# An attention-output stage put in a fixed order by hand, and snaps moved up in the down stage

## The chip, the cores and the metric

The kernel runs on one core of a Trainium2 chip. The metric is the device time of one execution in microseconds (us), lower is better. The timed figure is about 2 us more than the span of the profile of the same execution (757.7 against 755.9 for the kernel before), so spans are compared with spans and times with times. In the profile PE is TensorE (matrix multiplication), PEld its loading of weights, DVE is VectorE, ACT is ScalarE, POOL is GpSimd and SP is SyncE, which issues the data transfers (DMA).

## The reference, cut to what matters

```python
x = A_x                                   # 1 x 2048 x 1024, bf16
h = x + A(layernorm(x), wqkv, wo)         # attention block
out = h + B(layernorm(h), W_gate, W_up, W_down)

def A(x, wqkv, wo):                       # 32 heads of 32
    q, k, v = split(x @ wqkv)
    phi = lambda t: where(t > 0, t + 1, exp(t)) + 1e-6
    kv  = einsum("bhsd,bhse->bhde", phi(k), v);   z = sum(phi(k), s)
    num = phi(q) @ kv;   den = phi(q) @ z + 1e-6
    return concat_heads(num / den) @ wo

def B(x, Wg, Wu, Wd):                     # F = 3584
    g = x @ Wg;  h = relu(g) * (x @ Wu);  return h @ Wd
```

Attention is linear: for each token only a numerator and a denominator against one small matrix are needed, then a division, then the output projection.

## The kernel before

The large products (Q, K, V, gate, up, down) are done by the Strassen-Winograd scheme: seven products of half-size blocks in place of eight, with sums and differences of blocks on VectorE and copies of partial sums, here called snaps, that must be taken out of PSUM before TensorE may accumulate further into the same bank.

The attention-output stage works on 16 tiles of 128 tokens, in two halves of 8. For each tile it does the following steps.

- `nd`: 8 short matmuls of 132 columns, which yield numerators and denominators. They fill three PSUM banks, in pieces of 3, 3 and 2 matmuls.
- Ln and Exp on ScalarE give the reciprocal of the denominators, a multiplication on VectorE gives `o_sb` and so frees the bank.
- A DMA transposes `o_sb` into `oT`.
- `attn`: 16 matmuls of 512 columns, the output projection in two halves of 8. Each half needs one PSUM bank. VectorE adds the residual `x_res`.
- Layer norm on ScalarE, a DMA transpose of `hn`, and on VectorE the sums `hs` for Strassen.

The pool of PSUM banks is what ties these together: `nd` and `attn` share the same three banks (tag `"ab"`, `bufs=3`). The `nd` of one tile takes all three.

```python
    def strassen(pool, work, mm, fin, sbufs=3):          # a generator: 6 pieces
        ...
        for v in range(2):
            A[v] = pool.tile([P, NW], FP32, tag="A", bufs=2, name="Aq")
            mm(A[v], 1, v, True)
            snap(v, "m1")
        yield
        m2(0)
        for v in range(2):
            mm(A[v], 6, v, False)
            snap(v, "u2")
        m2(1)
        yield
        ...                                              # four more pieces

    def phi_end(dst, e):                                 # after phi_begin: dst = q + 1 + eps
        nc.scalar.activation(out=e, in_=dst, func=ACT.Exp, bias=negb[:, 0:1], scale=1.0)
        nc.vector.tensor_scalar(out=e, in0=e, scalar1=1.0, scalar2=PHI_EPS, op0=ALU.min, op1=ALU.add)
        nc.vector.tensor_tensor(out=dst, in0=dst, in1=e, op=ALU.max)

    # q_unit: one Exp, min and max for each 512 columns
        def fin(i, j, v, ps, m):
            dst = pqT[:, j * KH + c + v, i * HS + s * SW:i * HS + (s + 1) * SW]
            phi_begin(dst, ps, m)
            e = qw[-1].tile([P, NW], BF16, tag="e", name="e")
            phi_end(dst, e[:])

    # attn_stages(t)
        def nd():
            ...
            for c0, n in pieces:                         # 3, 3 and 2 of the 8
                ps = ndpool.tile([P, NW], FP32, tag="ab", name="nd")
                for c in range(c0, c0 + n):
                    nc.tensor.matmul(ps[:, (c - c0) * NDW:(c - c0 + 1) * NDW],
                                     lhsT=pqT[:, c, t * P:(t + 1) * P], rhs=kvz[:, c, :], start=True, stop=True)
                ...
                nc.scalar.activation(out=den[:, 0:n], in_=ndv[:, :, P:NDW], func=ACT.Ln, bias=deps[:], scale=1.0)
                nc.scalar.activation(out=rd[:, 0:n], in_=den[:, 0:n], func=ACT.Exp, scale=-1.0)
                nc.vector.tensor_tensor(out=ov[:, c0:c0 + n], in0=..., in1=rd..., op=ALU.mult)
        ...
        def wo_h():
            for j in range(2):
                ps = abpool.tile([P, NW], FP32, tag="ab", name="attn")
                for c in range(KC):
                    nc.tensor.matmul(ps[:], lhsT=st["oT"][:, c, :], rhs=wo_sb[:, c, j * NW:(j + 1) * NW],
                                     start=(c == 0), stop=(c == KC - 1))
                nc.vector.scalar_tensor_tensor(out=h_sb[:, j * NW:(j + 1) * NW], in0=ps[:], ...)   # residual
            ...                                          # layer norm

    for step in range(QSTEPS):                           # first half; Q of the second half between
        attn_step(step)
        ...
        for p in rest[step * len(rest) // QSTEPS:(step + 1) * len(rest) // QSTEPS]:
            next(p)
    ...                                                  # second half: pieces of four gate/up quads between

    # only here, ahead of the gate/up and down stages:
    ctx.enter_context(tc.manual_schedule(engines={ET.PE, ET.DVE, ET.Activation}))
```

The last line matters. Up to it the framework's scheduler decides the order of instructions on each engine; after it, the order of the program text is the order on TensorE, VectorE and ScalarE.

The down stage, which is in program order in both kernels, holds this (`pop()` issues one queued VectorE sum of operands for a later product, `s1`, `s2` and `s3` are the snaps, `prv` is the product before):

```python
            cur["m1"]()
            if prv:
                prv["11"]()
                pop()
            cur["s1"]()
            cur["m2"]()
            ...
            late_w()
            pop()
            cur["m6"]()
            if prv:
                prv["01"]()
            pop()
            ...
            cur["m5f" if tail else "m5"]()
            cur["s2"]()
```

Of the kernel before, what the change touches and what calls it, by code (L numbers as in the profile page):

```python
# [7 lines left out]
ACT = mybir.ActivationFunctionType  # L8
# [23 lines left out]
def block_kernel(ctx: ExitStack, tc: tile.TileContext, x, wqkv, wo, wg, wu, wd, out, H: int):  # L32
    nc = tc.nc
# [110 lines left out]
    def strassen(pool, work, mm, fin, sbufs=3):  # L144


        A, E, snaps = {}, {}, {}

        def snap(v, nm):
            if v == 0:  # L150
                snaps[nm] = work.tile([P, 2, NW], FP32, tag="snap", bufs=sbufs, name=nm)
            snaps[nm, v] = snaps[nm][:, v, :]
            nc.scalar.copy(out=snaps[nm, v], in_=A[v][:])  # L153

        def m2(v):
            d = pool.tile([P, NW], FP32, tag="D", bufs=1, name="Dq")
            mm(d, 2, v, True)
            fin(0, 0, v, d, snaps["m1", v])
# [4 lines that stand above are left out]
            snap(v, "m1")  # L163
        yield
        m2(0)
        for v in range(2):
            mm(A[v], 6, v, False)
            snap(v, "u2")
        m2(1)
        yield  # L170
        for v in range(2):
            E[v] = pool.tile([P, NW], FP32, tag="E", bufs=2, name="Eq")
            mm(E[v], 5, v, True)
        yield
        for v in range(2):
            mm(A[v], 7, v, False)
            snap(v, "u3")
            fin(1, 1, v, E[v], snaps["u3", v])
        yield
        for v in range(2):  # L180
            mm(A[v], 4, v, False)
            fin(1, 0, v, A[v], None)
        yield
        for v in range(2):
            mm(E[v], 3, v, False)
            fin(0, 1, v, E[v], snaps["u2", v])
        yield
# [242 lines left out]
    def q_unit(s, c):  # L430

        left = left_ops(xT[s], xS[s])
        ready = {}

        def mm(ps, m, v, start):
            for kc in range(KH):
                nc.tensor.matmul(ps[:], lhsT=rq[m - 1][:, kc, (c + v) * P:(c + v + 1) * P],
                                 rhs=left[m - 1][:, kc, :], start=(start and kc == 0),
                                 stop=(kc == KH - 1), skip_group_check=True)

        def fin(i, j, v, ps, m):
            dst = pqT[:, j * KH + c + v, i * HS + s * SW:i * HS + (s + 1) * SW]
            phi_begin(dst, ps, m)
            e = qw[-1].tile([P, NW], BF16, tag="e", name="e")
            phi_end(dst, e[:])

        return strassen(pspool, qw[-1], mm, fin)
# [47 lines left out]
    def attn_stages(t):  # L495
# [5 lines left out]
        def nd():  # L501
# [3 lines left out]
            ov = o_sb[:].rearrange("p (k h e) -> p k h e", k=KC, h=HPC)  # L505
            for c0, n in pieces:
                ps = ndpool.tile([P, NW], FP32, tag="ab", name="nd")
                for c in range(c0, c0 + n):
# [3 lines left out]
                den = bsmall.tile([P, GPB, HPC], FP32, tag="den", name="den")  # L512
                nc.scalar.activation(out=den[:, 0:n], in_=ndv[:, :, P:NDW], func=ACT.Ln, bias=deps[:], scale=1.0)
                rd = bsmall.tile([P, GPB, HPC], FP32, tag="rd", name="rd")
                nc.scalar.activation(out=rd[:, 0:n], in_=den[:, 0:n], func=ACT.Exp, scale=-1.0)  # L515
                nc.vector.tensor_tensor(  # L516
                    out=ov[:, c0:c0 + n], in0=ndv[:, :, 0:P].rearrange("p k (h e) -> p k h e", h=HPC),
                    in1=rd[:, 0:n, :].unsqueeze(3).to_broadcast([P, n, HPC, Dh]), op=ALU.mult)

        def oT():  # L520
            oT = bwork.tile([P, D], BF16, tag="oT", bufs=XB, name="oT")
            st["oT"] = oT[:].rearrange("p (c t) -> p c t", c=KC)
            nc.sync.dma_start_transpose(out=st["oT"], in_=st["o"][:])

        def x_in():
            x_sb = bwork.tile([P, D], BF16, tag="x_res", bufs=XB, name="x_res")
            nc.sync.dma_start(out=x_sb[:], in_=xf[t * P:(t + 1) * P, :])
            st["x"] = x_sb

        def wo_h():  # L530
            h_sb = st["x"]
            tot = bsmall.tile([P, 2], FP32, tag="tot", name="tot")
            for j in range(2):
                ps = abpool.tile([P, NW], FP32, tag="ab", name="attn")
                for c in range(KC):
                    nc.tensor.matmul(ps[:], lhsT=st["oT"][:, c, :], rhs=wo_sb[:, c, j * NW:(j + 1) * NW],  # L536
                                     start=(c == 0), stop=(c == KC - 1))
                nc.vector.scalar_tensor_tensor(out=h_sb[:, j * NW:(j + 1) * NW], in0=ps[:], scalar=1.0,  # L538
                                               in1=h_sb[:, j * NW:(j + 1) * NW], op0=ALU.mult, op1=ALU.add,
                                               accum_out=tot[:, j:j + 1])  # L540
            nc.sync.dma_start(out=h_dram[i][s][:, r // P, :], in_=h_sb[:])
            st["hn"] = bwork.tile([P, D], BF16, tag="hn", bufs=HB, name="hn")

            sm = bsmall.tile([P, 6], FP32, tag="sm", name="sm")
            nmean, var, lnv, rstd, nmr = (sm[:, i:i + 1] for i in range(5))
            nc.vector.tensor_scalar(out=nmean, in0=tot[:, 0:1], scalar1=tot[:, 1:2], scalar2=-1.0 / D,
                                    op0=ALU.add, op1=ALU.mult)
            nc.scalar.activation(out=st["hn"][:], in_=h_sb[:], func=ACT.Square, bias=nmean, scale=1.0, accum_out=var)
# [3 lines left out]
            nc.scalar.activation(out=st["hn"][:], in_=h_sb[:], func=ACT.Identity, bias=nmr, scale=rstd)  # L552

        def hn_T():
            nc.sync.dma_start_transpose(out=hnT[s][i][:, :, r:r + P], in_=st["hn"][:])

        return nd, oT, x_in, wo_h, hn_T

    LAG = (0, 1, 1, 2, 4)
    STS = ST // NS  # L560
    QSTEPS = STS + 0
    stages = [attn_stages(t) for t in order]
    begin_at = [n if n < STS else n - STS + QSTEPS for n in range(ST)]

    def attn_step(step):
        for k in range(len(LAG)):
            n = step - LAG[k]
            if n in begin_at:
                n = begin_at.index(n)
                stages[n][k]()  # L570
                if k == len(LAG) - 1 and n % STS >= NT:
                    left_sums(hnT[n // STS], hns[n // STS], slice(n % NT * P, (n % NT + 1) * P), nc.vector)

    rest = [p for s in range(1, NS) for c in range(0, KH, 2) for p in [q_unit(s, c)] * 6]
    for step in range(QSTEPS):
        attn_step(step)
        if step:
            for _ in range(-(-len(early_loads) // (QSTEPS - step))):
                early_loads.pop(0)(held[step][0:1, 0:1])
        for p in rest[step * len(rest) // QSTEPS:(step + 1) * len(rest) // QSTEPS]:  # L580
            next(p)
# [12 lines left out]
    def weight_sums(w_sb, fi, nm):  # L594
# [15 lines left out]
        return steps, lambda: (b[0][0], b[1][0], b[1][1], t[0][:, 3], t[0][:, 0], t[0][:, 1], t[0][:, 2])  # L610

    def run_sums(wt, fi):

        out = []
        for steps, ops in all_sums(wt, fi):
            for f in steps:
                f()
            out.append(ops())
        return out
# [66 lines left out]
    def early_quad(s, fc, w):  # L686
# [4 lines left out]
        def mm(ps, m, v, start):  # L691
            for kc in range(KH):
                nc.tensor.matmul(ps[:], lhsT=w[v][m - 1][:, kc, :], rhs=left[m - 1][:, kc, :],
# [16 lines left out]
        return strassen(pspool, mwork, mm, fin, 4)  # L710
# [5 lines left out]
    flow = []  # L716
    for f in range(NE):
        st = {}

        def begin(f=f, st=st):  # L720
            st["q"] = early_quad(0, f, run_sums(early[f // GP], f % GP))
            next(st["q"])

        flow += [begin] + [lambda st=st: next(st["q"])] * 5
    ready = STS + LAG[-1]
    for step in range(QSTEPS, ready):
        if step == QSTEPS:
            flow.pop(0)()
        attn_step(step)
    steps = QSTEPS + STS + LAG[-1] - ready  # L730
    for n in range(steps):
        attn_step(ready + n)
        for p in flow[n * len(flow) // steps:(n + 1) * len(flow) // steps]:
            p()
# [9 lines left out]
    ET = mybir.EngineType  # L744
    ctx.enter_context(tc.manual_schedule(engines={ET.PE, ET.DVE, ET.Activation}))

# [9 lines left out]
    def quad(s, fc, w, k):  # L756
# [10 lines left out]
        def m(n, nm, t=None):  # L767
# [3 lines left out]
            for v in range(2):  # L771
                for kc in range(KH):
                    nc.tensor.matmul(ps[:, v, :], lhsT=w[v][n - 1][:, kc, :], rhs=left[n - 1][:, kc, :],  # L773
# [89 lines left out]
    now = sums_of_run(0)  # L863
    for steps, _ in now:
        for f in steps:
            f()
    prv, k = None, 0
    for r, (wt, f, fi, toks) in enumerate(runs):
        w = [ops() for _, ops in now]
# [316 lines left out]
    for n in range(1, len(OUTER)):  # L1186
# [26 lines left out]
        if op["k"] in INNER:  # L1213
# [16 lines left out]
            pop()  # L1230
# [3 lines left out]
            pop()  # L1234
# [24 lines left out]
        else:  # L1259
            pss = []  # L1260
            for p in range(4):
                ps = acc(("A", "A", "XY"[(n + 1) % 2], "XY"[n % 2])[p])
                plain_mm(ps, n, p, 0)
                plain_mm(ps, n, p, 1)
                if p == 0 and prv:
# [7 lines left out]
                    load_h(op["k"], 1)  # L1273
                s, t0 = divmod(2 * p, NT)
# [4 lines left out]
                pop(2)  # L1279
# [50 lines left out]
```

## Time and profile before

| What | Kernel before |
|---|---|
| Time, median of 3 runs (range) | 755.6 us (755.51 to 757.81) |
| Span of the profile | 755.9 us, mean granted clock 0.993 |
| Attention-output stage, first `nd` to first gate/up quad after it | 147.2 to 298.0 us: 150.8 us |
| of which matmuls at their full pace | 592 x 0.2158 + 128 x 0.0592 = 135.3 us |
| of which lost | 15.4 us |

The pace comes from start to start of neighbouring matmuls in stretches without waits: 0.2158 us for 512 columns, 0.0592 us for 132 columns, 3.06 us for 28 of 256 columns. The end that the profile draws for a matmul is later than the start of the next, so a wait counted from start to start is 0.1 to 0.2 us longer than the idle time in brackets in the profile, and a group's length in the timeline is a little more than its cost.

The view of windows of the kernel before, by stage (attention output; gate/up quads; down). Columns are the window, its length, busy time and instruction count of each engine, then the granted TensorE clock, the DMA share and GB/s:

```profile
core 0: us, PE busy (x) PEld busy (x) DVE busy (x) ACT busy (x) POOL busy (x), PEclk, DMA share, GB/s
147.20:297.98 150.78, 139.48 (x707) 65.54 (x720) 113.37 (x293) 103.38 (x268) 1.50 (x8) 0.99 0.66 162
297.98:590.00 292.02, 290.75 (x1329) 132.35 (x1353) 221.53 (x406) 124.76 (x167) 0.00 (x0) 1.00 0.55 173
590.00:755.90 165.90, 157.10 (x1194) 118.55 (x1194) 127.45 (x108) 4.83 (x6) 0.00 (x0) 0.98 0.69 244
```

The middle stage has a clock of 1.00 and no gaps (290.75 of 292.02 us). The losses lie in the other two. The view of waits of TensorE in the kernel before says for what (total us, times, longest):

```profile
PE accA L1105 <- DVE snap L1111: 4.8, 2, 2.6
PE attn L536 <- DVE o_sb L516: 3.3, 7, 0.9
```

Two things in the timeline matter. First, how the attention stage hides the latency of the division (start, length, engine, line, operation, and in brackets the idle time before and its releaser):

```profile
155.74 0.63 PE L509 MATMUL nd<-kvz,pq_mem 128*128 128x132 bf16 x8
156.21 1.24 PE L437 MATMUL Aq<-xT,wq_sb 128*128 128x512 f16 x5
157.31 3.61 PE L536 MATMUL attn<-wo_mem,oT 128*128 128x512 bf16 x15
```

After the eight matmuls of `nd` the scheduler put five matmuls of Q (`Aq`), which need nothing of `nd`. When they are done a bank is free, and the projection starts with no wait. Secondly, the down stage has two gaps like this one:

```profile
626.73 4.88 PE L1105 MATMUL accA<-w,xd 128*128 128x256 f16 x28 [2.11 <-DVE snap L1111]
631.45 3.22 PE L1105 MATMUL accA<-wd,x 128*128 128x256 f16 x28
```

TensorE waits 2.11 us for the snap, and the 28 matmuls after the wait take 631.45 - 626.73 = 4.72 us from start to start in place of 3.06. They have the same form as the 28 after them; the clock is not the same (the view of windows gives 0.50 from 626.90 to 630.32 us, and 1.00 on both sides). The Trainium skill, "TensorE: Matmul & The Clock Gate", Part 1, says that a TensorE that was idle for a window of about 3.4 us runs at half rate, until it has been busy for about 3.4 us. The trace agrees with the half rate and with the time to warm up. The page (section "Wait — 56ns, not 53.3ns?") gives the cold pace as the number of columns over 1.2 GHz, which is 0.213 us for 256 columns by estimate, 0.104 us more than the measured 3.06 / 28 = 0.109. The excess of 4.72 - 3.06 = 1.66 us is then 16 slow matmuls, an estimate from that page's figure, and these take 16 x 0.213 = 3.4 us, as long as the trace's stretch at 0.50. The second such wait, near 732 us, was 2.64 us, with the same 4.72 us after it.

### The profile page before, as it was taken

The numbers are of one execution on the slowest core, as the hardware profiler recorded it, in microseconds if no ns is written. First come the engines' busy times: TensorE is split into PE (matmuls) and PEld (weight loads), VectorE is DVE, ScalarE is ACT, GpSimd is POOL, SyncE is SP. The second block draws the span as 40 slices with busy tenths as digits, with TensorE's granted clock in tenths as the row PEclk, the third lists the DMA queues.
The fourth block names the chain that finished last, engine by engine and source line by source line (L and its number), as shares of the span: only waits on it lengthen the run. The fifth ranks groups of instructions, "written<-read, shape, count | busy, mean of one in ns | idle before, by whom it ended". The sixth has DMA issues, their size and how long they took to land. (4 is left out here: it accounts for less than half of the span.)

```text
span 755.9 us, 10599 instructions
## 1 busy us (share of the span) xinstructions
PE 727.9 (96%) x3967; PEld 384.2 (51%) x4020; DVE 568.2 (75%) x1023; ACT 324.7 (43%) x596; POOL 5.9 (1%) x44
## 2 busy tenths in 40 slices
PE   8999999999889989999999999999999998999987
PEld 3444555444344434444444444444444477888556
DVE  6997654876886766778778787887776398995695
ACT  4785653878767644444344444434344110000000
POOL 0000000000000000000000000000000000000000
PEclk9999999999999999999999999999999999999999
DMA  9756003089857526165638368585482596987722
GB/s 321 167 125 153 0 1 112 1 188 218 186 144 178 135 74 202 35 185 140 200 110 237 112 194 252 194 253 179 144 302 96 189 385 244 360 295 281 238 98 56
DMA packets 146579, 132.03 MB, mean 175 GB/s; under 512 B 50912, under 2 KB 128096, under 8 KB 146528
## 3 DMA queue, kind: packets, MB, share of 16 engines
q1 hardware_dynamic: 135392, 123.23, 53.7%
q10 hardware_dynamic: 11136, 8.13, 3.4%
q8 instruction: 31, 0.51, 0.3%
q14 instruction: 20, 0.16, 0.1%
HBM read 79.95 MB, written 39.85 MB: 158 GB/s over the span
## 5 line engine op out<-in xcount | busy, mean ns | idle before, releaser
L783 ACT ACTIVATE gu<-gu 128x512 bf16<-128x512 bf16 x72 | 45.4, 630 | 131.7 <-DVE gu L782 127.3
L778 ACT COPY snap<-accA 128x1024 f32<-128x1024 f32 x72 | 72.4, 1008 | 37.1 <-PE accA L773 37.1
L536 PE MATMUL attn<-wo_mem,oT 128*128 128x512 bf16 x247 | 58.7, 385 | 4.1 <-DVE o_sb L516 3.3
L773 PEld LDWEIGHTS <-tg 128*128 128x128 f16 x384 | 37.6, 98 | 45.3
L773 PEld LDWEIGHTS <-tu 128*128 128x128 f16 x384 | 37.6, 98 | 45.3
L782 DVE TENSOR_TENSOR gu<-accY,snap 128x1024 bf16<-128x1024 f32 x36 | 43.9, 1219 | 9.8 <-ACT snap L778 9.8
L153 ACT COPY u<-Aq 128x512 f32<-128x512 f32 x56 | 32.3, 582 | 44.0 <-PE Aq L297 20.4
L782 DVE TENSOR_TENSOR gu<-accX,snap 128x1024 bf16<-128x1024 f32 x36 | 43.8, 1218 | 7.3 <-PE accX L773 4.7
L773 PE MATMUL accA<-hn,tg 128*128 128x512 f16 (+1 forms) x192 | 49.3, 379 | 0.0
L773 PE MATMUL accA<-hn,tu 128*128 128x512 f16 (+1 forms) x192 | 49.3, 379 | 0.0
L1105 PEld LDWEIGHTS <-x 128*128 128x128 f16 (+1 forms) x448 | 43.8, 98 | 5.5
L773 PEld LDWEIGHTS <-wg 128*128 128x128 bf16 x288 | 28.2, 98 | 34.9 <-issue 1.1
L773 PEld LDWEIGHTS <-wu 128*128 128x128 bf16 x288 | 28.2, 98 | 34.0
L536 PEld LDWEIGHTS <-oT 128*128 128x128 bf16 x256 | 25.3, 99 | 36.0 <-issue 8.5
L1105 PEld LDWEIGHTS <-xs 128*128 128x128 f16 x280 | 28.2, 101 | 6.7 <-issue 2.8
L297 PEld LDWEIGHTS <-xT 128*128 128x128 bf16 (+1 forms) x192 | 18.6, 98 | 24.5 <-issue 3.2
L786 DVE TENSOR_TENSOR hq<-gu 128x512 bf16<-128x512 bf16 x48 | 20.3, 422 | 14.3 <-ACT gu L783 14.2
L516 DVE TENSOR_TENSOR o_sb<-nd,rd 128x384 bf16<-128x384 f32 (+1 forms) x48 | 22.8, 506 | 8.6 <-ACT rd L515 7.5
L1111 DVE TENSOR_TENSOR snap<-accA,u 128x1024 f32<-128x1024 f32 x16 | 19.5, 1218 | 11.1 <-PE accA L1105 11.1
L538 DVE SCALAR_TENSOR_TENSOR x_res<-attn,x_res 128x512 bf16<-128x512 f32 x32 | 22.0, 688 | 7.6 <-PE attn L536 7.5
L934 PEld LDWEIGHTS <-x 128*128 128x128 bf16 (+1 forms) x168 | 16.4, 98 | 19.8
L773 PE MATMUL accA<-hn,wg 128*128 128x512 bf16 x73 | 23.3, 379 | 2.0 <-DVE gu L702 0.8
(232 smaller groups left out, 1417.0 us busy)
## 6 DMA issues: line engine op xcount, KB each, us to landing
x<-x_dram SPq DMA_DIRECT2D x17, 896.0 KB, 8.4
x_dram<-hq SPq DMA_DIRECT2D x28, 512.0 KB, 3.0
wg<-in_B_W_gate_dram SPq DMA_DIRECT2D x14, 512.0 KB, 5.2
wu<-in_B_W_up_dram SPq DMA_DIRECT2D x14, 512.0 KB, 7.5
wraw<-in_B_W_down_dram SPq DMA_DIRECT2D x14, 512.0 KB, 4.9
x_dram<-hq SPq DMA_DIRECT2D x28, 256.0 KB, 2.4
t_dram<-wt SPq DMA_DIRECT2D x28, 256.0 KB, 2.3
xd<-x_dram SPq DMA_DIRECT2D x6, 896.0 KB, 6.5
```

The costliest lines, as they stand in the source:

```text
L153: nc.scalar.copy(out=snaps[nm, v], in_=A[v][:])
L297: nc.tensor.matmul(ps[:], lhsT=left[m - 1][:, kc, r + v * P:r + (v + 1) * P], rhs=right[m - 1][:, kc, :], start=(start and kc == 0), stop= ...
L516: nc.vector.tensor_tensor(out=ov[:, c0:c0 + n], in0=ndv[:, :, 0:P].rearrange("p k (h e) -> p k h e", h=HPC), in1=rd[:, 0:n, :].unsqueeze(3 ...
L536: nc.tensor.matmul(ps[:], lhsT=st["oT"][:, c, :], rhs=wo_sb[:, c, j * NW:(j + 1) * NW], start=(c == 0), stop=(c == KC - 1))
L538: nc.vector.scalar_tensor_tensor(out=h_sb[:, j * NW:(j + 1) * NW], in0=ps[:], scalar=1.0, in1=h_sb[:, j * NW:(j + 1) * NW], op0=ALU.mult, ...
L773: nc.tensor.matmul(ps[:, v, :], lhsT=w[v][n - 1][:, kc, :], rhs=left[n - 1][:, kc, :], start=(t is not None and kc == 0), stop=(kc == KH - ...
L778: nc.scalar.copy(out=st[nm][:], in_=halves(st["A"]))
L782: add(out=g[:], in0=halves(st[nm]), in1=st[base][:], op=ALU.add)
L783: nc.scalar.activation(out=g[:, 0, :], in_=g[:, 0, :], func=ACT.Relu)
L786: add(out=out[q], in0=st[q][:, 0, :], in1=st[q][:, 1, :], op=ALU.mult)
L1105: nc.tensor.matmul(pv[:, tt, :], lhsT=left(m)[:, f, tt * P:(tt + 1) * P], rhs=right(m)[:, f, :], start=(t is not None and f == 0 and tt % ...
L1111: add(out=st[nm][:], in0=view("A"), in1=base[s][:, :, cols(j)], op=ALU.add)
```

## The change

Four things change, and all aim at TensorE's gaps.

1. The order of TensorE, VectorE and ScalarE is fixed by hand from the attention-output stage on, by a function `attn_steps`. Projection halves, pieces of Q and pieces of four gate/up quads alternate, and the Strassen pieces are finer (8 in place of 6).
2. The Exp of the reciprocal is one instruction for all three Ln of a tile, in place of three.
3. The phi of Q works on pairs of 512 columns: one Exp, min and max on 1024 columns.
4. In the down stage queued operand sums go behind the snap, and not ahead of it.

```diff
     def q_unit(s, c, fine=False):
...
-            dst = pqT[:, j * KH + c + v, i * HS + s * SW:i * HS + (s + 1) * SW]
-            phi_begin(dst, ps, m)
-            e = qw[-1].tile([P, NW], BF16, tag="e", name="e")
-            phi_end(dst, e[:])
+            pair = pqT[:, j * KH + c:j * KH + c + 2, i * HS + s * SW:i * HS + (s + 1) * SW]
+            phi_begin(pair[:, v], ps, m)
+            if v == 1:
+                e = qw[-1].tile([P, 2, NW], BF16, tag="e", name="e")
+                phi_end(pair, e[:])
... (nd)
-                nc.scalar.activation(out=den[:, 0:n], in_=ndv[:, :, P:NDW], func=ACT.Ln, ...)
-                nc.scalar.activation(out=rd[:, 0:n], in_=den[:, 0:n], func=ACT.Exp, scale=-1.0)
+                nc.scalar.activation(out=den[:, c0:c0 + n], in_=ndv[:, :, P:NDW], func=ACT.Ln, ...)
+                views.append(ndv)
+            nc.scalar.activation(out=rd[:], in_=den[:], func=ACT.Exp, scale=-1.0)
+            for (c0, n), ndv in zip(pieces, views):
                 nc.vector.tensor_tensor(out=ov[:, c0:c0 + n], ...
... (steps: "nd", "wo" by halves, "a" and "b" the layer norm, "h" the sums hs)
+    ctx.enter_context(tc.manual_schedule(engines={ET.PE, ET.DVE, ET.Activation}))
+
+    def attn_steps(n0, fills, between):
+        ...
+        for n in range(n0 + 1, n0 + STS):
+            do(n, "nd")
+            do(n - 2, "a")
+            do(n - 2, "b")
+            between(n - n0)
+            do(n - 1, "wo", 0)
+            fill()
+            do(n - 3, "h")
+            do(n - 1, "wo", 1)
+            extra = len(fills) - 4 - (n0 + STS - 1 - n)
+            fill(-(-extra // (n0 + STS - n)) if extra > 0 else 0)
...
+    stages[0]["nd"]()
+    for _ in range(4):
+        q_fill.pop(0)()
+    attn_steps(0, q_fill, early_load)
... (second half)
+    for _ in range(2):
+        flow.pop(0)()
+    stages[STS]["nd"]()
+    stages[STS - 1]["h"]()
+    for _ in range(2):
+        flow.pop(0)()
+    attn_steps(STS, flow, lambda n: None)
... (down stage)
             late_w()
-            pop()
+            if prv:
+                pop()
             cur["m6"]()
             if prv:
                 prv["01"]()
-            pop()
+                pop()
...
                 plain_mm(ps, n, p, 0)
-                plain_mm(ps, n, p, 1)
                 if p == 0 and prv:
                     prv["11"]()
 ...
+                    pop()
+                plain_mm(ps, n, p, 1)
...
-                pop(2)
+                pop(2 if p < 3 else 0)
```

## The prediction

> **What bounds it now.** TensorE: busy 727.9 of 755.9 us (the page). So only its gaps matter, and they lie in two places (timeline of TensorE). (1) Attention output, 147.2 to 298.0 us: at the measured pitches (0.216 us per 512-column matmul, 0.059 per 132-column one) its 592 + 128 matmuls are 135 us; the stage takes 150.7, so 15 us are lost. (2) The down stage: two waits for a VectorE "snap" (624.5 and 732.1 us). Each group after them (28 matmuls) takes 4.7 us instead of 3.06: the half-rate cold clock of the Trainium skill, "TensorE: Matmul & The Clock Gate", Part 1 (granted clock 0.91 and 0.93 in those windows). Together about 2.3 + 1.7 + 2.8 + 1.7 = 8.4 us.
>
> **Down stage.** Moving operand sums behind the snap lets the snap start when its matmuls end. I count both waits as gone: -8.4 us, VectorE keeping about 1 us of margin.
>
> **Attention stage.** The order is now strict on TensorE, VectorE and ScalarE. In it every nd (8 short matmuls, 0.47 us) is followed at once by half of an output projection, which needs a PSUM bank that the same nd has just filled (three banks, nd takes all three). In the trace nd to freed bank takes 1.6 to 1.9 us (Ln 0.27, Exp 0.20, multiply 0.55), and now Exp waits for all three Ln. Before, Q or gate/up matmuls filled that time; now nothing does. 14 tiles x 1.4 us = 20 us. That alone exceeds the 15 us lost now. In addition (estimates from trace durations):
> - the first nd stands before any Q of the second half and waits for the last phi pair, whose exp, min and max are now 1.15 + 0.42 + 0.69 us behind other exps: 3.5 us;
> - tiles 1 and 2: their Ln stands behind a phi exp that waits for VectorE: 2 us more each;
> - tiles 3 to 7: nd waits for the eviction (0.69 us, sometimes behind a phi pair) of the projection just before it: 0.6 to 1.8 us each, 5 us;
> - change of halves: relu, Ln, Exp and multiplies stand ahead of the hn sums that the first quad's third product needs: 6 to 8 us;
> - second half: copies behind relus, hand-over to the quads: 4 us.
> Sum about 43 us of gaps instead of 15; some overlap: stage +20 to +33 us. The pairwise phi saves some 5 us of VectorE and ScalarE, off the critical path. Quads from 300 to 590 us are unchanged.
>
> **Time.** 755.6 - 8.4 + about 30 = 778 us; 80% range 762 to 792. Faster by over 2%: 0.03; within 2%: 0.25; slower by over 2%: 0.72.
>
> **What would show it.** Waits of the attn matmuls for o_sb (3.3 us now) rise to 20 us or more; waits of nd for pq_mem and x_res rise; the first all-double-bank quad starts 20 to 33 us later than 298.0; TensorE busy in that stage falls from 92% to about 80%; the snap waits of the down stage (4.8 us) vanish, and the time from the last quad to the end shrinks by about 8 us.
>
> **What would make it wrong.** If ScalarE and VectorE run well ahead, only the 1.4 us per tile remains: about 760. If gaps let the clock drop often, it is worse than 790. If operand loads (DMA share 0.84 in the down stage) come too late, part of the 8.4 us is lost.

## More of the kernel before

The page of the profile of the kernel before says that TensorE is busy nearly all the time (busy us, share of the span, number of instructions):

```profile
PE 727.9 (96%) x3967; PEld 384.2 (51%) x4020; DVE 568.2 (75%) x1023; ACT 324.7 (43%) x596; POOL 5.9 (1%) x44
```

This figure alone says little of how well TensorE is used. The Trainium skill, "Perfetto Trace Analysis", section "Identifying the Most-Contended Engine", says that matmul busy share is not a good measure of the distance to the roofline.

## The result, and the profile after

The changed kernel takes 804.5 us, the median of 4 runs (801.34 to 808.32), against 755.62 us (755.51 to 757.81). The ratio is 1.065, with a 95% interval of 1.060 to 1.069. A ratio here is the mean time of one kernel's fast runs over that of the other's of the same rounds, so not quite the ratio of the medians that are quoted. The direction of the prediction was right; the time lies 12 us above the upper end of its range.

| What | Before | After |
|---|---|---|
| Time, median | 755.6 us | 804.5 us |
| Span, mean granted clock | 755.9 us, 0.993 | 800.5 us, 0.981 |
| Attention-output stage | 150.8 us | 203.35 us |
| From there to the end | 457.9 us | 449.55 us |

The page after, the line of busy time:

```profile
PE 737.8 (92%) x4020; PEld 385.6 (48%) x4020; DVE 568.2 (71%) x991; ACT 325.9 (41%) x548; POOL 5.7 (1%) x44
```

Both kernels have the same matmuls, and TensorE is busy for longer in the slower one. So a larger busy time is not a better use of TensorE here. (Some 50 of 4020 matmul records are missing from the trace of the kernel before, which accounts for a part of the difference.) The view of windows after, by the same stages and with the same columns:

```profile
147.60:350.95 203.35, 151.32 (x721) 68.82 (x720) 113.50 (x269) 105.39 (x226) 1.35 (x8) 0.92 0.47 110
350.95:643.00 292.05, 292.05 (x1354) 132.42 (x1354) 223.28 (x411) 124.89 (x168) 0.00 (x0) 1.00 0.57 180
643.00:800.50 157.50, 153.52 (x1196) 116.80 (x1194) 127.50 (x108) 4.80 (x6) 0.00 (x0) 1.00 0.73 257
```

The middle stage is unchanged (292 us). The down stage has lost its gaps and runs at clock 1.00. All of the loss is in the attention stage, where TensorE is busy for 74% of the time (151.32 of 203.35) in place of 92.5%, and the granted clock is 0.92 in place of 0.99. The view of waits of TensorE after:

```profile
PE attn L540 <- DVE o_sb L524: 27.2, 14, 3.8
PE nd L517 <- DVE pq_mem L205: 6.9, 2, 3.5
PE Aq L724 <- DVE hs L118: 5.4, 1, 5.4
PE nd L517 <- DVE x_res L542: 4.7, 5, 1.7
```

The snap waits are gone. The wait of the projection for `o_sb` is 27.2 us in 14 times, in place of 3.3 in 7. The timeline after, with all engines, shows one of the longest of these from its beginning, `nd` of the second tile:

```profile
158.55 0.63 PE L517 MATMUL nd<-kvz,pq_mem 128*128 128x132 bf16 x8
158.82 0.69 DVE L198 SCALAR_TENSOR_TENSOR pq_mem<-Dq,m 128x512 bf16<-128x512 f32 x1 [1.90 <-PE Dq L441]
...
159.55 1.15 ACT L203 ACTIVATE e<-pq_mem,negb 128x1024 bf16<-128x1024 bf16 x1 [1.08 <-DVE pq_mem L198]
160.60 0.57 ACT L520 ACTIVATE den<-nd,deps 128x12 f32<-128x12 f32 x3
...
161.19 0.69 DVE L205 TENSOR_TENSOR pq_mem<-pq_mem,e 128x1024 bf16<-128x1024 bf16 x1
161.21 0.23 ACT L522 ACTIVATE rd<-den 128x32 f32<-128x32 f32 x1
161.80 1.35 DVE L524 TENSOR_TENSOR o_sb<-nd,rd 128x384 bf16<-128x384 f32 x3
162.41 1.86 PE L540 MATMUL attn<-wo_mem,oT 128*128 128x512 bf16 x4 [3.22 <-DVE o_sb L524]
```

It is read from top to bottom. The `nd` matmuls end at about 159.2 us. ScalarE could then take the Ln, but in the fixed order a phi Exp of 1024 columns stands ahead of it, and this one itself waits for VectorE's sum (158.82). It runs from 159.55 for 1.15 us. The three Ln come at 160.60, the joint Exp at 161.21. VectorE meanwhile finishes the phi pair (min 0.43, max 0.69) and multiplies at 161.80; the bank is free after the first of the three multiplies, and TensorE goes on at 162.41. Its next work in the program, 8 matmuls of Q, was not held up by anything but its place: in the run e3 below the same 8 start right after `nd`. Here they stood behind the projection, and the Trainium skill, "PSUM — Partial Sum Buffer", section "Engine vs sequencer instructions", says that matmuls start and complete in program order. The trace agrees: 3.22 us of idleness, and the Q matmuls start after the projection.

What such a wait costs beyond itself is seen in TensorE's own timeline after:

```profile
162.41 3.25 PE L540 MATMUL attn<-wo_mem,oT 128*128 128x512 bf16 x8 [3.22 <-DVE o_sb L524]
165.49 1.89 PE L441 MATMUL Eq<-xS,tq 128*128 128x512 f16 x8
167.22 1.89 PE L540 MATMUL attn<-wo_mem,oT 128*128 128x512 bf16 x8
```

The 8 projection matmuls after the wait take 165.49 - 162.41 = 3.08 us; the 8 of Q after them take 167.22 - 165.49 = 1.73 us, which is the normal pace. Not every wait has this cost. At the end of the stage TensorE waits 2.37 us for VectorE, and the next four matmuls take 351.81 - 350.95 = 0.86 us, their normal pace:

```profile
350.95 1.02 PE L818 MATMUL accA<-hn,wg 128*128 128x512 bf16 x4 [2.37 <-DVE gu L733]
351.81 1.03 PE L818 MATMUL accA<-hn,wu 128*128 128x512 bf16 x4
```

The same wait in the run e7 below (2.36 us) is followed by 12 matmuls that take 4.27 us in place of 2.59. What differs is when it comes. In the 13 traces (all but e5's) the granted clock changes only at points of a grid of 3.413 us. The view of windows on that grid, first after and then e7 (window, length, PE busy and instructions, granted clock, DMA share, GB/s):

```profile
346.11:349.52 3.41, 2.47 (x12) 1.00 0.29 74
349.52:352.94 3.42, 1.99 (x10) 1.00 0.84 232
352.94:356.35 3.41, 3.41 (x18) 1.00 1.02 250
```

```profile
339.51:342.92 3.41, 1.05 (x6) 1.00 0.72 160
342.92:346.33 3.41, 3.41 (x10) 0.50 0.97 280
```

In after the wait lies across two stretches of the grid; in e7 most of it lies in one, and the next stretch runs at half clock. In the 13 traces every full-clock stretch in which TensorE was busy, as drawn, for less than 0.39 of the time is followed by one at half clock, and none with more than 0.43 is; between the two both occur. So what counts is how much of a wait falls into one stretch, and that is partly luck, worth up to 1.7 us here. This is read from the traces; no run was made to test it.

The change of the halves looks like this in TensorE's timeline after:

```profile
244.62 0.40 PE L517 MATMUL nd<-kvz,pq_mem 128*128 128x132 bf16 x2 [3.42 <-DVE pq_mem L205]
250.44 1.89 PE L724 MATMUL Aq<-hs,tg 128*128 128x512 f16 x4 [5.42 <-DVE hs L118]
252.13 1.91 PE L724 MATMUL Aq<-hs,tu 128*128 128x512 f16 x4
```

`nd` of the first tile of the second half waits 3.42 us for the last phi pair of Q. Then the first gate/up quad's third product waits 5.42 us for `hs`, the Strassen sums of the last tile of the first half. In the fixed order those sums stand on VectorE behind weight sums, a gate/up addition and the multiplies of `o_sb`, and the multiplies wait for ScalarE's Ln and Exp. The four matmuls after that wait take 252.13 - 250.44 = 1.69 us, 0.42 us each and so nearly twice 0.2158: here the half rate is seen matmul by matmul.

The down stage after is without gaps:

```profile
674.37 3.22 PE L1147 MATMUL accY<-ws,xd 128*128 128x256 f16 x28
677.43 3.22 PE L1147 MATMUL accA<-w,xd 128*128 128x256 f16 x28
```

The sum is this, with waits taken from start to start out of the timeline of TensorE:

| Attention stage | Before | After |
|---|---|---|
| Matmuls at their full pace | 135.3 us | 135.3 us |
| `attn` waits for `o_sb` | 4.5 (7 times) | 29.4 (14 times) |
| `nd` waits for `pq_mem` (phi) | 2.4 | 7.2 |
| `nd` waits for `x_res` (eviction of the projection) | 1.9 | 5.5 |
| `Aq` waits for `hs` | 0 | 5.6 |
| Other waits | 3.9 | 9.0 |
| Slow clock (what is left) | 2.8 | 11.3 |
| Sum | 150.8 us | 203.3 us |

So of 52.6 us, 44.1 are waits and 8.5 slow clock. Together with the 8.4 us gained later, this is the difference of the spans within 0.5 us.

### The profile page after: what moved, and what is told of

The parts are those of the page before. It is cut to its first block, busy times and chain, and to the rows that moved or that the text cites. A ratio compares the mean times of both kernels' runs of the same rounds, so it can differ in the third digit from the quotient of the medians.

```text
span 800.5 us, 10551 instructions
## 1 busy us (share of the span) xinstructions
PE 737.8 (92%) x4020; PEld 385.6 (48%) x4020; DVE 568.2 (71%) x991; ACT 325.9 (41%) x548; POOL 5.7 (1%) x44
## 4 chain that ended last, share of the span: by engine, by line
PE 56%; DVE 0%; issue 0%
PE accA L818 21%; PE accY L818 8%; PE accX L818 8%; PE accA L1147 8%; PE accA L976 3%; PE accX L1147 3%; PE accY L1147 2%; PE accX L976 2%; PE accY L976 2%; PE accY L1173 0%; PE accX L1173 0%; DVE gu L733 0%; DVE o L1111 0%; DVE tu L645 0%
## 5 line engine op out<-in xcount | busy, mean ns | idle before, releaser
L540 PE MATMUL attn<-wo_mem,oT 128*128 128x512 bf16 x256 | 66.7, 409 | 28.3 <-DVE o_sb L524 27.2
```

## The experiments

The main theory was that the fixed order itself is the loss: `nd` and the projection stand next to each other, so the latency of the division is exposed, and the rest are waits of the same sort at the edges, each with slow matmuls after it. Rivals were that finer pieces, pairing or the joint Exp are to blame, or that the attention part and the down part are not independent. Twelve runs were made, of eleven kernels (e12 repeats e5). All gave correct results, and all runs were in the fast state but for one of e5, which is named there. "After" is the changed kernel and "before" the kernel before. Before was run with each group of experiments and had a median of 754.63 to 756.12 us there.

| Run | Median us (range) | Ratio to before, 95% interval |
|---|---|---|
| e1_down_only | 748.63 (747.46 to 749.27) | 0.990 (0.988 to 0.993) |
| e2_attn_only | 812.93 (811.41 to 814.17) | 1.076 (1.074 to 1.078) |
| e3_fill_first | 780.47 (779.13 to 782.79) | 1.033 (1.031 to 1.036) |
| e4_warm | 797.98 (796.97 to 798.38) | 1.056 (1.054 to 1.058) |
| e5_phi_single | 808.67 (806.11 to 808.84) | 1.070 (1.068 to 1.073) |
| e6_exp_split | 801.82 (800.06 to 805.14) | 1.064 (1.061 to 1.067) |
| e7_edges | 794.85 (793.17 to 797.85) | 1.053 (1.050 to 1.056) |
| e8_all_fixed | 776.75 (776.39 to 777.64) | 1.029 (1.027 to 1.031) |
| e9_scheduled | 756.92 (755.60 to 757.37) | 1.002 (1.000 to 1.004) |
| e10_pair_down | 748.05 (747.03 to 749.85) | 0.991 (0.989 to 0.993) |
| e11_fixed_paired | 775.83 (774.36 to 778.26) | 1.028 (1.025 to 1.031) |
| e12_phi_single_again | 806.15 (806.06 to 806.24) | 1.068 (1.065 to 1.071) |

### e1_down_only: the down part alone, on the kernel before

The edit is the last third of the diff above, `if prv: pop()` and the moved sinks, applied to before.

> The kernel before with only the down-stage reordering of the change. Theory (two VectorE snaps came late, each wait of 2.3 to 2.8 us was followed by a cold clock of 1.7 us): 755.6 - 8.4 = 747 us, both waits of TensorE for the snap gone, and the time from the first quad of the middle stage to the end 8.4 us shorter, as in the changed kernel. Rival (part of the 8.4 us seen in the changed kernel comes from DMA having run further ahead there, since its first half was slower): a gain of 4 us or less here, with new waits in the down stage.

It took 748.63 us, 7 us less than before and 1% faster. Both snap waits are gone from the view of waits, and the granted clock rose to 0.997. The theory held. The spans differ by 8.5 us (755.9 and 747.4), and from the first quad of the middle stage to the end it is 449.5 us, 8.4 less than before, as expected. That is more than the waits alone (4.8 us): the rest is the slow matmuls that no longer follow them.

### e2_attn_only: the attention part alone

The edit undoes the down part in after.

> The changed kernel with the down-stage reordering undone. If the two halves of the change add up, 804.5 + 8.4 = about 813 us, and the two snap waits are back. If the down stage gains only by itself, 804 us.

It took 812.93 us, 8.4 us more than after. The two parts add up: 748.6 + 812.9 - 755.6 = 805.9 against 804.5 measured. The rival that they interact falls.

### e3_fill_first: the piece of other work ahead of the projection

```diff
             between(n - n0)
-            do(n - 1, "wo", 0)
             fill()
+            do(n - 1, "wo", 0)
             do(n - 3, "h")
```

> The changed kernel with one line moved: in each step the piece of Q or of a gate/up quad comes between nd and the first half projection, instead of between the two halves. Theory (the loss is nd's bank being asked back at once, strict order, nothing to fill the wait): the 14 waits of attn for o_sb fall from 27 us to under 10 us and most cold-clock groups go; about 775 us (765 to 785). Rival (the loss lies in longer ScalarE and VectorE work: pairwise phi and one Exp for three Ln): unchanged within 3 us of 804.

It took 780.47 us, so 24 us of the 49 come back by moving one line. The waits for `o_sb` fell from 27.2 to 6.9 us; the wait for the transposed `oT` rose from 1.0 to 3.4 us, and the others of the stage stayed within 0.6 us. The granted clock of the stage rose only from 0.92 to 0.94, so most of the slow matmuls stayed, against the expectation. The timeline of TensorE in this run, at the same tile as above, shows why:

```profile
157.31 0.63 PE L517 MATMUL nd<-kvz,pq_mem 128*128 128x132 bf16 x8
157.78 1.89 PE L441 MATMUL Eq<-xS,tq 128*128 128x512 f16 x8
161.16 3.61 PE L540 MATMUL attn<-wo_mem,oT 128*128 128x512 bf16 x15 [1.50 <-DVE o_sb L524]
```

The 8 matmuls of Q now run during the division. What remains is 1.50 us, because this tile's Ln still stands behind the phi Exp. This run shows directly that a large part of the loss, 24 us, is the neighbourhood of `nd` and `attn`, and not the amount of work on VectorE or ScalarE, which is the same.

### e4_warm: useless matmuls in the long waits

To measure the slow clock by itself, 93 matmuls of 512 columns that no result uses (the expectation says 92) were put into the long waits of after. They write the PSUM bank of tag `"D"`, which the product `Dq` of Strassen also uses and which is free in most of these waits.

```diff
+    def spin_mm(count):
+        if count:
+            sp = pspool.tile([P, NW], FP32, tag="D", bufs=1, name="spin2")
+            for _ in range(count):
+                nc.tensor.matmul(sp[:], lhsT=kvz[:, 0, 0:P], rhs=wo_sb[:, 0, 0:NW], start=True, stop=True)
...
+            spin_mm({1: 12, 2: 16, 3: 5, 4: 5, STS: 14, STS + 5: 12}.get(order.index(t), 0))
             nc.scalar.activation(out=rd[:], in_=den[:], func=ACT.Exp, scale=-1.0)
```

(15, 7 and 7 more stand ahead of the third piece of `nd` of the tiles 0, 3 and 4.)

> The changed kernel plus useless matmuls (92 of 512 columns, about 20 us of TensorE work) placed in the longest waits of tiles 0 to 4, 8 and 13, shorter than each wait, into a bank that is free then; results unchanged. Theory (about 12 us of the loss is the clock at half rate after long waits, a cost of its own, which my prediction left out): granted clock back above 0.99 in that stage and about 794 us, faster with more work. Rival (the slow matmul groups after the waits are slow for another reason, operands or weights arriving late): the same slow groups remain and the time is 804 us or more.

It took 797.98 us, about 6 us less than after with 93 x 0.2158 = 20.1 us more of matmuls. The timeline of TensorE in this run, at the same tile:

```profile
158.43 2.75 PE L504 MATMUL spin<-wo_mem,kvz 128*128 128x512 bf16 x11 [0.39 <-DVE pq_mem L198]
161.26 1.89 PE L549 MATMUL attn<-wo_mem,oT 128*128 128x512 bf16 x8
162.99 1.89 PE L441 MATMUL Eq<-xS,tq 128*128 128x512 f16 x8
```

From `nd` (157.41 in this run) to the projection it is 3.85 us, and 3.86 in after (158.55 to 162.41), so the wait was not shortened, only filled. The projection's 8 matmuls then take 1.73 us in place of 3.08. In the first half of the stage all the slow groups went, and the half took 82.8 us in place of 90.5, so there the slow clock cost about 7.7 us. At the change of halves there was no gain: the useless matmuls waited 1.8 us themselves, for VectorE to read `Dq` out of their bank, and ran slowly (14 in 4.8 us). So the clock of the whole stage was 0.96, not above 0.99, and the time 4 us more than expected. That the slow clock is a cost of its own, in addition to the waits, is shown.

### e5_phi_single and e12_phi_single_again: phi on 512 columns again

```diff
-            phi_begin(pair[:, v], ps, m)
-            if v == 1:
-                e = qw[-1].tile([P, 2, NW], BF16, tag="e", name="e")
-                phi_end(pair, e[:])
+            phi_begin(dst, ps, m)
+            e = qw[-1].tile([P, NW], BF16, tag="e", name="e")
+            phi_end(dst, e[:])
```

> The changed kernel with the pairwise phi undone (exp, min and max on 512 columns again). Theory (a minor part: the pair sits on the chain only where an nd waits for the phi just before it, at the first nd, tiles 1 to 4 and the change of halves, some 0.4 to 1 us each): 3 to 6 us faster than 804.5, so 799 to 801. Rival (pairing is a main cause): 15 us or more faster. Second rival (pairing saves time, as was intended): slower than 806.

It was not faster than after: 806.11 to 808.84 us. One run of the four took 1138 us at a clock of 0.65 and is left out, and the profile fell into that one, so the kernel was run again.

> The same kernel as the run with phi undone, whose profile fell in a slow state, for a profile in the fast state. Expected where that run was slower than the changed kernel by about 4 us: copies of u behind an exp on ScalarE (waits of Q matmuls for u up by 1 to 2 us) and longer waits for x_res behind the extra VectorE instructions; the waits for o_sb of tiles 1 and 2 about 0.4 us shorter each.

It took 806.15 us, with a profile at a clock of 0.977. The waits for `o_sb` were 27.0 us in sum, the same as in after. I had expected that a shorter Exp ahead of the Ln would shorten the waits of the tiles 1 and 2. It did for tile 1, from 3.22 to 2.40 us; that of tile 2 grew from 3.77 to 4.29, and the gain was gone. More groups after waits ran slowly than in after; of the 4.0 us between the two spans 1.7 lie behind the stage, where the wait of 2.37 us was followed by slow matmuls here and not in after. In the trace an Exp of 512 columns takes 0.72 us and one of 1024 columns 1.15 us. The Trainium skill, "Perfetto Trace Analysis", section "Optimizing Scalar/DVE Operations", says that larger operations save overhead where an engine is saturated, and that breaking instructions up may let work finish sooner where an engine that isn't saturated causes bubbles elsewhere. The saving of overhead agrees with this trace (1.15 against 2 x 0.72 us); a gain from breaking up the phi did not appear. The medians differ from after by 2 to 4 us to the worse, but the intervals of the ratios overlap, so pairing gains at most a little in the fixed order. It is not a cause of the loss.

### e6_exp_split: one Exp for each Ln again

```diff
-                views.append(ndv)
-            nc.scalar.activation(out=rd[:], in_=den[:], func=ACT.Exp, scale=-1.0)
+                nc.scalar.activation(out=rd[:, c0:c0 + n], in_=den[:, c0:c0 + n], func=ACT.Exp, scale=-1.0)
+                views.append(ndv)
```

> The changed kernel with one Exp after each Ln again, instead of one Exp for all three. Theory: the first multiply, which frees the bank asked for, need not wait for the third piece of nd; tiles 3 to 7 wait about 0.65 instead of 1.27 us for o_sb, the others 0.2 to 0.4 us less: 4 to 8 us faster, about 798. Rival (six small ScalarE instructions per tile cost as much as they save): 803 to 806.

The waits fell where expected: those of the tiles 3 to 7 from 1.26 us to between 0.49 and 0.92 (one gave way to a wait of 0.81 for `oT`), and all waits for `o_sb` from 27.2 to 22.8 us. The median fell by 2.7 us, less than expected and not clear of noise (801.82 us, and the interval of the ratio overlaps that of after). A part of the shorter waits came back as longer waits of `nd` for `pq_mem` (7.4 us in place of 6.9) and for the transposed `oT` (1.9 in place of 1.2, start to start). So the joint Exp is a small term.

### e7_edges: the first `nd` of each half later

```diff
-    stages[0]["nd"]()
-    for _ in range(4):
+    for n in range(4):
+        if n == 2:
+            stages[0]["nd"]()
         q_fill.pop(0)()
...
-    stages[STS]["nd"]()
     stages[STS - 1]["h"]()
-    for _ in range(2):
+    flow.pop(0)()
+    stages[STS]["nd"]()
+    for _ in range(2):
         flow.pop(0)()
```

> The changed kernel with two moves of order: the first nd two pieces of Q later, and at the change of halves the hn sums before the first nd of the second half, that nd one piece later. Theory (three waits of 3.5, 3.4 and 5.4 us and the cold clock after them stand there only because of the order): the two waits of nd for pq_mem go, the wait for the hn sums falls below 2 us; 10 to 15 us faster, about 792. Rival (these waits only move to the next instruction, since ScalarE and VectorE are late at both places): less than 5 us faster, above 799.

It took 794.85 us, 10 us less than after. The waits of `nd` for `pq_mem` fell from 6.9 to 1.4 us as expected. The wait for `hs`, which was to fall below 2 us, rose from 5.4 to 6.7:

```profile
235.90 1.03 PE L725 MATMUL Dq<-hn,wg 128*128 128x512 bf16 x4
243.67 1.89 PE L725 MATMUL Aq<-hs,tg 128*128 128x512 f16 x4 [6.75 <-DVE hs L118]
```

At the change of halves the `nd` wait and the `hs` wait became one wait of 6.75 us. From the piece before it to the product it is 7.8 us (235.90 to 243.67) in place of 10.6 in after (239.82 to 250.44), so about a quarter of it has gone and the rest has moved. The chain behind it, ScalarE and VectorE handing the last phi of Q back and forth, was not touched by this edit. In the profiled runs (spans of 793.6 and 800.5 us) 3.9 us were gained up to the first gate/up piece (234.17 against 238.10 us) and 4.7 us from it to the end of the stage; 1.7 us were lost again behind it, to the half clock shown above.

### e8_all_fixed and e11_fixed_paired: all repairs together, in the fixed order

e8 is the edits of e3, e5, e6 and e7 together; e11 is the same with pairs kept.

> All four edits of the changed kernel together: piece between nd and the first half projection, phi single, one Exp per Ln, both edges moved. If the named causes are the whole loss of the attention stage: 780.5 (first edit alone) less 12 (edges), 4 (phi), 4 (Exp): about 761 us, with waits of TensorE in that stage under 15 us. If a large cause is still unnamed: 770 or more. Not expected to beat the down-stage part alone (748.6).

> The changed kernel with three edits of order and Exp (piece between nd and the first half projection, one Exp per Ln, both edges moved) and the pairs kept. If undoing the pairs is what spoiled the run with all four edits (776.8): 771 to 773 us, with smaller waits of nd for x_res. If the edits do not add up for another reason: 776 or more.

They took 776.75 and 775.83 us. Both miss, and the second misses although the phi pairs were back, so it isn't the phi that spoils the sum. Added up from the single runs, e3, e6 and e7 would give 804.5 - 24.0 - 2.7 - 9.7 = 768 us. The view of waits of e11 shows what stands in the way:

```profile
PE nd L517 <- DVE x_res L542: 6.2, 7, 3.1
PE attn L540 <- DMA oT<-o_sb: 6.1, 4, 2.8
```

The waits for `x_res` and for the DMA that transposes `o_sb` were 4.7 and 1.0 us in after and are 6.2 and 6.1 us here. With the earlier waits gone, TensorE comes sooner to the next step of the same chain, one tile later, and waits there. This is read from the waits alone; no run took these two waits away by themselves. With all repairs the fixed order is still 28 us behind e10.

### e9_scheduled: everything of the change but the fixed order in the attention stage

```diff
     ET = mybir.EngineType
-    ctx.enter_context(tc.manual_schedule(engines={ET.PE, ET.DVE, ET.Activation}))

     def attn_steps(n0, fills, between):
...
+    ctx.enter_context(tc.manual_schedule(engines={ET.PE, ET.DVE, ET.Activation}))
     def acc(tag):
```

> The changed kernel with one thing undone: in the attention stage the order on TensorE, VectorE and ScalarE is again left to the scheduler (strict order begins at the down stage, as before). Pairwise phi, one Exp per tile, split projections, finer pieces and the down-stage part all stay. Theory (the strict hand order is nearly the whole loss, the other parts are small): 745 to 760 us, the waits for o_sb below 8 us. Rival (the finer pieces, the joined Exp or the pairs cost much whatever the order): 775 us or more.

It took 756.92 us: 47.6 us are back with the finer pieces, the joint Exp, the split halves and the pairs all in place. The attention part costs 804.5 - 748.6 = 55.9 us (after against e1), so this is 85% of it. The waits of `attn` for `o_sb` are 0.5 us. The timeline of TensorE in this run:

```profile
161.28 0.52 PE L517 MATMUL nd<-kvz,pq_mem 128*128 128x132 bf16 x6
...
163.25 1.89 PE L441 MATMUL Eq<-xS,wq_sb 128*128 128x512 f16 x8
...
165.63 3.62 PE L540 MATMUL attn<-wo_mem,oT 128*128 128x512 bf16 x15
```

Between the `nd` at 161.28 (and its two matmuls of the third piece, left out here) and the projection at 165.63 the scheduler has put Q matmuls, although the program text has the projection directly after `nd`. This separates the parts: this fixed order is most of the loss. (Not any fixed order: e3 is fixed too and loses 24 us less.) What remains is the difference between 757 and the 748.6 of e1: the stage takes 158.2 us here and 150.8 in before. `nd` now waits 3.8 us for `o_sb`, which it does not in before, and the granted clock of the stage is 0.97 in place of 0.99. Whether that is the finer pieces, the joint Exp, the split halves, or simply other choices of the scheduler, was not separated.

### e10_pair_down: the down part and the pairs, on the kernel before

> The kernel before with the down-stage part and the pairwise phi, nothing else. Theory (pairing saves ScalarE and VectorE time that is not on the chain when the scheduler may fill): within 3 us of the down-stage part alone (748.6), so 746 to 751. Rival (undoing it in the changed kernel cost 4 us, so it is a gain of its own): 745 or less.

It took 748.05 us against 748.63 for e1; the ranges overlap. Pairing is neutral where the scheduler orders the stage. e1 and e10 are the best versions: both are 1% faster than before and 7% faster than after.

## Why the prediction was wrong

The prediction was 778 us with a range of 762 to 792, and the time is 804.5. The direction and the mechanism were right; the size was not.

- **"I count both waits as gone: -8.4 us."** Right. From the first quad to the end the span shrank from 457.9 to 449.55 us, by 8.4. e1 shows it alone (-7 us) and e2 by its absence (+8.4).
- **The fixed order puts `attn` directly behind `nd` and exposes the division.** Right in kind. e3 and e9 show it: moving one piece of work between them takes away 20 of the 27 us of these waits, and giving the order back to the scheduler leaves 0.5 us of them (and 3.8 us of `nd` for `o_sb`).
- **"14 tiles x 1.4 us = 20 us", and 2 us more each for tiles 1 and 2.** 24 us predicted, 29.4 measured. The longest waits were right (3.2 and 3.8 us), tiles 3 to 7 also (1.3), but in the second half they were 1.6 to 2.0 us and once 3.2, since there relus and copies of the quads stand ahead of the Ln: at 269.25 us in after a relu of 0.63 us does, at 314.55 us a relu and a copy.
- **The other waits.** First `nd` 3.5 predicted, 3.7 measured; change of halves 6 to 8 against 10.7 (1.55 + 3.57 + 5.58), because I counted the `hs` wait and left the wait of the second half's first `nd` for phi out; `x_res` 5 against 5.5; copies and hand-over 4 against 6.2; the transposed `oT` 0 against 1.2.
- **"Sum about 43 us of gaps instead of 15; some overlap: stage +20 to +33 us."** This is the step that failed. The gaps were 56.7 us from start to start, and nothing overlapped: each wait stood by itself in TensorE's order. The stage grew by 52.6 us. The 15 us that I took off as the gaps of before were 12.6 of waits and 2.8 of slow clock.
- **The slow clock.** I used it for the down stage and did not put it in the sum for the attention stage; it stood only in the last paragraph, as a risk. It cost 11.3 us there in place of 2.8. e4 shows that it is a cost beside the waits.

Measured against the prediction, the terms of the stage add up to 56.7 + 11.3 = 68.0 us lost, where I had 43. Of the 25 us that were missing, 14 are waits that I took too small and 11 the slow clock that I left out.

- **"The pairwise phi saves some 5 us of VectorE and ScalarE, off the critical path."** Right as far as the runs can tell: e10 shows no effect under the scheduler, and e5 and e12 differ from after by no more than 2 to 4 us, with overlapping intervals.
- **"TensorE busy in that stage falls from 92% to about 80%."** It fell to 74%, with the slow matmuls counted as busy.

## What to carry to other kernels

If you fix the order of an in-order engine by hand, look for each step whose result frees the buffer that the next step needs, and put independent work between the two; here one moved line was worth 24 us of 49. Count a gap on TensorE as longer than it is: in before and after every gap of 2.6 us or more in the two stages studied here, and some shorter ones, was followed by slow matmuls that cost up to another 1.7 us. It is no rule of the gap's length: in e11 a wait of 3.09 us (at 176.21 us) was followed by full pace. And test a change of many parts by its parts, since here one part was worth -8 us and was hidden under another that cost +57.

## What the Trainium skill lacked or had wrong

- "TensorE: Matmul & The Clock Gate", Part 1, has TensorE go cold after an idle window of about 3.4 us. Here a wait of 2.11 us was enough for 28 matmuls to take 4.72 us in place of 3.06, and so were gaps of 1.68 and 1.26 us with two short matmuls between them (184.1 and 185.7 us in after; the next 8 matmuls took 3.37 us in place of 1.73). On the other hand a wait of 2.37 us at the end of that stage was followed by matmuls at full pace. So the length of a single wait doesn't decide it in these traces, and a window need not be idle throughout. The page gives no share of busy time that is too little: in these traces it lies between 0.39 and 0.43 of a stretch of 3.41 us, with TensorE's busy time as the profile draws it. The half rate (0.42 us for 512 columns after the wait of 5.42 us) and the 3.4 us of warming up (the stretches at 0.50) agree with the traces.

- The same page, "Loop structure matters more than you think", marks VectorE's copy out of PSUM as something that does not break TensorE's warmth, in a loop whose next matmuls follow at once. Here the next matmuls had to wait for VectorE and ScalarE, because they share three banks with the matmuls before: 27.2 us of waits for `o_sb`, and a clock of 0.92 in the stage.
- "Perfetto Trace Analysis", "Optimizing Scalar/DVE Operations", says that breaking instructions up may let work finish sooner. Splitting the phi left the waits for `o_sb` at 27.0 us against 27.2 (e12). Splitting the Exp took 4.4 us of waits away, and the median fell by 2.7 us, not clear of noise (e6). That section does not speak of the order on the engine, which was worth more here (24 us in e3).
- No page that I read puts a number on what a hand-fixed order may lose against the framework's scheduler: here 47.6 us of 804.5 (e9).
